# A fused attention and max-out kernel: two PSUM pools to the end, one two-term product instead of three, and new engine shares in the head

## The chip, the cores and the metric

One core of a Trainium2 chip runs the kernel. The metric is the time of one execution on the device, in microseconds (us); the profile's span is some 1.8 us shorter, because it counts from the first to the last instruction. All executions told of here count as fast: none was over 1.5% above the fastest of its kernel. TensorE is called PE, VectorE DVE, ScalarE ACT and GpSimd POOL in the profile's lines.

## The reference

```python
x, state: (8, 8, 512, 64), (8, 8, 32, 64)      # batch, head, sequence, depth
a     = softmax(x @ state^T / 8);   xread = a @ state        # (8, 8, 512, 64)
a2    = softmax(state @ x^T / 8);   sread = a2 @ x           # (8, 8, 32, 64)
X     = concat([xread, sread], sequence), heads side by side # (8 * 544, 512)
out   = maximum(X @ w1, X @ w2) @ w_out                      # w1, w2: (512, 1024), w_out: (1024, 512)
```

The kernel uses two identities. With max(h1, h2) = relu(h1 - h2) + h2, the output is relu(X (W1 - W2)) W_out + X (W2 W_out). And xread = a @ state, so X W = a (state W): for each batch a small matrix SW = state [W1 - W2 | W2 W_out], of 1536 columns in three chunks of 512, replaces the large products. "Layer 1" is aT against the first two chunks with a relu; "layer 2" is aT against the third chunk plus the relu's result against W_out.

## The kernel before

Batch 0 runs while the weights still land. W1 - W2 must be made from fp32 data; where it is not ready, the kernel computes state W1 + (-state) W2 as a product in two terms. Batches 1 to 7 are a steady loop. The parts that matter (cuts marked with #...):

```python
    pools = dict(ps=early.enter_context(tc.tile_pool(name="ps", bufs=4, space=bass.MemoryType.PSUM)),
                 acc=early.enter_context(tc.tile_pool(name="acc", bufs=4, space=bass.MemoryType.PSUM)))
    def one_ring():
        early.close()
        pools["ps"] = pools["acc"] = ctx.enter_context(tc.tile_pool(name="ring", bufs=8, space=bass.MemoryType.PSUM))
#...
    load_states(first)
    load_x(0)
    for ch in range(2):
        load_w(w2f, moe_w2, ch)
        load_wo(2 * ch)
        load_wo(2 * ch + 1)
    load_w(w1f, moe_w1, 0)
    load_w(w1f, moe_w1, 1)
    load_x(1)
    load_states(slice(3, 8))
    load_x(2)
#...
    def sw_mm(b, ch, engs="VA"):
        pg = [bank(), bank()]
        two = b < TWO and ch < 2 and (b, ch) != (1, 0)
        terms = ((sbd, w1b), (sneg, w2b)) if two else ((sbd, wcat),)
#...                                   the head, from W1's second half on
    w_cast(w1b, w1f, 1)
    compact_x(1, 0)
    compact_x(1, 1)
    d_xt(1)
    cast_x(1)
    w_sub(2)
    w_sub(3)
    cast_states("P", rest)
    load_x(3)
    sT = d_states(rest)
    l2_add(0, 0, range(0, 4))
    u_sw(0, 1)
    for c in range(1, NC):
        l2_add(0, c, range(0, 4))
    l1(0, {}, range(4, 8))
    u_sc(1, 0, nc.vector)
    u_sc(1, 1, nc.gpsimd)
    cast_x(2)
    l2_add(0, 0, range(4, 8))
    l2_close(0, 0)
    u_sw(1, 0)
    l2_add(0, 1, range(4, 8))
    l2_close(0, 1)
    u_sw(1, 1)
    u_sr(1)
    compact_x(2, 0)
    compact_x(2, 1)
    l2_add(0, 2, range(4, 8))
    l2_close(0, 2)
    u_at(1, "V")
    l2_add(0, 3, range(4, 8))
    l2_close(0, 3)
    d_xt(2)
    u_sw(1, 2)
    u_srt(1)
    l2_out(0)
    one_ring()
    for b in range(1, B):
        #... steady loop: l1(b), l2(b), and batch b + 1's work between
```

`compact_x` casts x to bf16 on ScalarE, `d_xt` transposes it by DMA, `u_sc` is scores, Exp and normalisation, `u_at` the transpose of the attention weights with its copy out of PSUM (aT), `u_sw(b, ch)` one chunk of SW with its copies (swt), one half on VectorE and one on ScalarE.

The softmax here doesn't subtract the row's maximum and nothing guards it: scores larger than these inputs give would overflow.

## Time and profile before

| | before |
|---|---|
| time, median of the 6 executions beside the changed kernel | 152.12 us (151.97 to 152.38) |
| span of the profiled execution | 150.1 us |
| x of batch 1 landed / its transpose landed | 27.85 / 34.25 us |
| layer 1 of batch 1 starts | 41.94 us |
| a steady batch | 13.97 us (41.94 to 55.91) |

The prediction below shows and reads the main lines. One more, of the view of what each engine waited for, up to 42 us (who, for whom, us in total, times, longest):

```profile
PE ps L311 <- ACT sread_t L68: 0.8, 1, 0.8
```

L311 is layer 1. PE waits there because the two PSUM pools are closed and one pool of eight banks is opened, and the new pool's first bank waits for the old pools' last users.

### The profile page before, as it was taken

Reading aid. Unit: us, or ns where it says so; the run is one execution under the profiler, and the core shown is the slowest. Engines: PE = TensorE matmul, PEld = TensorE weight load, DVE = VectorE, ACT = ScalarE, POOL = GpSimd, SP = SyncE. Lnnn points to the kernel's source line nnn. Section 1 sums busy time; section 2 is a strip of 40 time slices with the busy share of each in tenths; the row PEclk is TensorE's granted clock in tenths of the full one; section 3 lists DMA queues with packets and bytes.
Section 4 is the critical chain, followed back from the end, with each engine's and each line's share of the span. In section 5 each row is a group of like instructions: output and inputs, shape, how many; then the busy total and the mean of one; then the engine's idle time right before and its main releaser. Section 6 shows DMA issues by size and latency. Waiting matters only on the chain.

```text
span 150.1 us, 3012 instructions
## 1 busy us (share of the span) xinstructions
PE 140.0 (93%) x1235; PEld 68.3 (45%) x1255; DVE 82.3 (55%) x151; ACT 75.6 (50%) x126; POOL 43.9 (29%) x44
## 2 busy tenths in 40 slices
PE   6769999999889999999999999999999999999990
PEld 1357643343435445434544444445445434764460
DVE  5378648428968187716854582658067625721120
ACT  3066339927869147727844683478167136521000
POOL 3025119994843520550064017104100500000000
PEclk9977999999999999999999999999999999999999
DMA  4999999989699867974979397851596030502423
GB/s 97 367 392 388 388 384 328 302 157 280 91 273 286 229 127 242 309 148 76 294 265 198 121 292 216 158 226 55 107 109 279 0 74 37 242 0 70 141 105 109
DMA packets 37934, 29.89 MB, mean 199 GB/s; under 512 B 24864, under 2 KB 33312, under 8 KB 37024
## 3 DMA queue, kind: packets, MB, share of 16 engines
q1 hardware_dynamic: 37776, 29.56, 68.9%
q8 instruction: 10, 0.16, 0.4%
q10 hardware_dynamic: 144, 0.13, 0.3%
q14 instruction: 4, 0.03, 0.1%
HBM read 15.20 MB, written 8.91 MB: 161 GB/s over the span
## 4 chain that ended last, share of the span: by engine, by line
PE 70%; DMA 13%; SPq 7%; ACT 3%; DVE 2%; issue 1%
PE acc L326 31%; PE ps L311 16%; DMA xf<-in_x_dram 10%; PE acc L322 8%; SPq L102 4%; SPq L105 3%; PE ps L283 3%; DMA xt<-xc 3%; PE ps L370 2%; PE acc L380 2%; PE ps L221 2%; PE ps L244 1%; PE acc L360 1%; ACT xc L68 1%; PE acc L378 1%
## 5 line engine op out<-in xcount | busy, mean ns | idle before, releaser
L326 PE MATMUL acc<-wo,r 128*128 128x512 bf16 x238 | 57.8, 379 | 0.6 <-issue 0.2
L326 PEld LDWEIGHTS <-r 128*128 128x128 bf16 x248 | 23.9, 98 | 28.8 <-issue 0.6
L301 DVE TENSOR_SCALAR r<-ps 128x512 bf16<-128x512 f32 x32 | 22.1, 692 | 16.3 <-PE ps L311 16.1
L311 PE MATMUL ps<-aT,swt 128*128 128x512 bf16 x127 | 29.0, 379 | 1.0 <-ACT sread_t L68 0.8
L231 POOL TENSOR_TENSOR a<-e,er 128x512 bf16<-128x512 bf16 x13 | 13.4, 1048 | 54.2 <-ACT e L224 27.1
L70 DVE COPY ob<-acc 128x512 f32<-128x512 f32 (+1 forms) x17 | 11.1, 653 | 30.2 <-PE acc L326 29.8
L68 ACT COPY ob<-acc 128x512 f32<-128x512 f32 (+1 forms) x16 | 9.1, 572 | 28.6 <-PE acc L326 18.9
L299 ACT ACTIVATE r<-ps 128x512 bf16<-128x512 f32 x32 | 19.2, 601 | 8.3 <-PE ps L311 7.7
L68 ACT CAST swt<-ps 128x512 bf16<-128x512 f32 x24 | 12.9, 593 | 12.3 <-PE ps L283 12.2
L311 PEld LDWEIGHTS <-swt 128*128 128x128 bf16 x128 | 12.1, 98 | 15.3 <-DVE swt L70 1.3
L322 PE MATMUL acc<-swt,aT 128*128 128x512 bf16 x56 | 16.7, 380 | 0.8 <-issue 0.8
L72 POOL CAST xp<-xf 128x2048 bf16<-128x2048 f32 (+1 forms) x8 | 14.1, 1768 | 10.2 <-DMA xf<-in_x_dram 10.2
L70 DVE CAST swt<-ps 128x512 bf16<-128x512 f32 x24 | 15.3, 681 | 1.8 <-PE ps L283 1.7
L68 ACT CAST xc<-xf 128x1024 bf16<-128x1024 f32 x14 | 13.9, 1051 | 0.1
L228 DVE TENSOR_REDUCE es<-e 128x16 f32<-128x512 bf16 x16 | 10.6, 662 | 1.8 <-ACT e L224 1.8
L389 POOL TENSOR_TENSOR wcat<-w1f,w2f 128x1024 bf16<-128x1024 f32 x4 | 9.8, 2473 | 3.0 <-DMA w1f<-in_moe_w_dram 3.0
L224 ACT ACTIVATE e<-ps 128x512 bf16<-128x512 f32 x16 | 8.8, 595 | 1.3 <-PE ps L221 0.6
L322 PEld LDWEIGHTS <-aT 128*128 128x128 bf16 x62 | 4.7, 98 | 6.0 <-issue 2.6
L136 PE MATMUL ps<-warm 128*128 128x512 bf16 x14 | 6.0, 568 | 1.5 <-POOL warm L122 1.3
L415 PE MATMUL acc<-wo,w2t 128*128 128x512 bf16 x31 | 7.2, 379 | 0.1
L283 PE MATMUL ps<-wcat,sbd 64*32 64x512 bf16 x168 | 6.7, 380 | 0.1
L221 PEld LDWEIGHTS <-xt 128*128 128x128 bf16 x128 | 5.0, 101 | 2.9 <-DMA xt<-xc 0.6
(68 smaller groups left out, 104.5 us busy)
## 6 DMA issues: line engine op xcount, KB each, us to landing
xf<-in_x_dram SPq DMA_DIRECT2D x8, 1024.0 KB, 7.6
out_dram<-ob SPq DMA_DIRECT2D x7, 1024.0 KB, 5.0
w2f<-in_moe_w_dram SPq DMA_DIRECT2D x2, 1024.0 KB, 10.0
wof<-in_moe_w_out_dram SPq DMA_DIRECT2D x4, 512.0 KB, 11.3
w1f<-in_moe_w_dram SPq DMA_DIRECT2D x2, 1024.0 KB, 15.3
out_dram<-ob SPq DMA_DIRECT2D x3, 256.0 KB, 2.2
out_dram<-obs SPq DMA_DIRECT2D x8, 64.0 KB, 1.7
s_f<-in_state_dram SPq DMA_DIRECT2D x1, 320.0 KB, 13.8
```

The costliest lines, as they stand in the source:

```text
L68: nc.scalar.copy(o, i)
L70: nc.vector.tensor_copy(o, i)
L72: nc.gpsimd.tensor_copy(o, i)
L228: nc.vector.tensor_reduce(d["es"][:, g], d["e"][:, g].rearrange("p i c n -> p (i c) n"), axis=mybir.AxisListType.X, op=ALU.add)
L231: mul.tensor_mul(d["a"][:, g].rearrange("p c i n -> p i c n"), d["e"][:, g], d["er"][:, g].rearrange("p (i c) -> p i c", i=4).unsqueeze(3) ...
L283: nc.tensor.matmul(pg[g][32 * i:32 * i + 32, :], sneg[gs, b, i, :] if k else sbd[gs, b, 2 * i + g, g, :], w[gs, i, ch * 512:(ch + 1) * 512 ...
L299: nc.scalar.activation(out=o, in_=p, func=ACTF.Relu)
L301: nc.vector.tensor_scalar(o, p, scalar1=0.0, scalar2=None, op0=ALU.max)
L311: nc.tensor.matmul(p, SW[b][:, g, f * 128:(f + 1) * 128], AT[b][:, g, :], start=(g == 0), stop=(g == 1))
L322: nc.tensor.matmul(OB[b][1 + c], AT[b][:, g, c * 128:(c + 1) * 128], SW[b][:, g, FF:WC], start=(g == 0), stop=False)
L326: nc.tensor.matmul(OB[b][1 + c], R[b][:, f, c * 128:(c + 1) * 128], wo[:, f, :], start=False, stop=(f == NF - 1))
L389: nc.gpsimd.tensor_sub(wcat[:, :, cs], w1f[:, :, cs], w2f[:, :, cs])
```

## The change

Its intent is to take work off the head: fewer two-term products on PE, a shorter way from W1's landing to the first SW chunk, VectorE instead of the busy GpSimd for W1b's subtraction, no closing of the pools, more warm-up matmuls so that the clock stays up, and x of batch 0 in two pieces so that casts start earlier. Its core:

```diff
-    pools = dict(ps=early..., acc=early...)         # and one_ring(), all of it
+    pools = {k: ctx.enter_context(tc.tile_pool(name=k, bufs=4, space=bass.MemoryType.PSUM)) for k in ("ps", "acc")}
-    load_x(0)
+    load_x(0, 2)
-        pg = [bank(), bank()]
-        two = b < TWO and ch < 2 and (b, ch) != (1, 0)
+        pg = [bank(kind="acc" if ch == 2 and b > 1 else "ps") for g in range(2)]
+        two = (b, ch) == (0, 0)
#... the head: casts dealt anew, warm_up 6+9+2+2+3+1+2 matmuls instead of 6+5+1+3
-    w_cast(w1b, w1f, 0)
+    for e, i in (("V", slice(0, 2)), ("A", slice(2, 3)), ("P", slice(3, 4))):
+        copy(e, w1b[:, i, 0:512], w1f[:, i, 0:512])
#...
-    w_cast(w1b, w1f, 1)
+    w_sub(2, nc.vector)
+    w_sub(3, nc.vector)
#...
     l2_add(0, 2, range(4, 8))
     l2_close(0, 2)
+    u_sw(1, 2)
     u_at(1, "V")
-    l2_add(0, 3, range(4, 8))
-    l2_close(0, 3)
-    d_xt(2)                     # now right after compact_x(2, 1)
-    u_sw(1, 2)
-    u_srt(1)
+    l2_add(0, 3, range(4, 6))
+    u_srt(1)
+    l2_add(0, 3, range(6, 8))
+    l2_close(0, 3)
     l2_out(0)
-    one_ring()
```

More of the change, by code (lines that the diff above doesn't have):

```diff
@@ L40 @@
     assert D == 64 and Ns == 32 and S == 512 and H == 8 and DM == 512 and B % 4 == 0
-    TWO = 2
     WC = FF + DM
@@ L49 @@
     big = ctx.enter_context(tc.tile_pool(name="big", bufs=2))
-    early = ctx.enter_context(ExitStack())
-    pools = dict(ps=early.enter_context(tc.tile_pool(name="ps", bufs=4, space=bass.MemoryType.PSUM)),
-                 acc=early.enter_context(tc.tile_pool(name="acc", bufs=4, space=bass.MemoryType.PSUM)))
+    pools = {k: ctx.enter_context(tc.tile_pool(name=k, bufs=4, space=bass.MemoryType.PSUM)) for k in ("ps", "acc")}
     ctx.enter_context(tc.manual_schedule())
@@ L60, in acc @@
         return bank(kind="acc")
-    def one_ring():
-        early.close()
-        pools["ps"] = pools["acc"] = ctx.enter_context(tc.tile_pool(name="ring", bufs=8, space=bass.MemoryType.PSUM))
     def copy(eng, o, i):
@@ L125 @@
     nc.vector.memset(sbd, 0.0)
-    sneg = consts.tile([128, TWO, 4, Ns], BF16)
+    sneg = consts.tile([128, 4, Ns], BF16)
     wo = consts.tile([128, NF, DM], BF16)
     wcat = consts.tile([128, 4, WC], BF16)
-    w1b = stage.tile([128, 4, FF], BF16)
+    w1b = stage.tile([128, 4, 512], BF16)
     w2b = stage.tile([128, 4, FF], BF16)
@@ L167, in negate_states @@
             gs = slice(64 * g, 64 * g + 64)
-            negate("V", sneg[gs], sbd[gs, 0:TWO, g::2, g, :])
+            negate("V", sneg[gs], sbd[gs, 0, g::2, g, :])
     sread_t = consts.tile([128, 4, B * Ns], BF16)
@@ L283, in sw_mm @@
                     nc.tensor.matmul(pg[g][32 * i:32 * i + 32, :],
-                                     sneg[gs, b, i, :] if k else sbd[gs, b, 2 * i + g, g, :],
+                                     sneg[gs, i, :] if k else sbd[gs, b, 2 * i + g, g, :],
                                      w[gs, i, ch * 512:(ch + 1) * 512],
@@ L384, in moe_sread, with w_sub @@
                 nc.sync.dma_start(out=out[b * L + S:(b + 1) * L], in_=ob[32 * q:32 * q + 32, t, :])
-    def w_sub(q):
+    def w_sub(q, eng=nc.gpsimd):
         cs = slice(q * 256, (q + 1) * 256)
-        nc.gpsimd.tensor_sub(wcat[:, :, cs], w1f[:, :, cs], w2f[:, :, cs])
+        eng.tensor_sub(wcat[:, :, cs], w1f[:, :, cs], w2f[:, :, cs])
     def w_cast(o, w, ch, engs="VA"):
@@ L415, in w_wo, with w_wo_out @@
             nc.tensor.matmul(WO[i], w2t[:, i, f, :], wo[:, f, :], start=(f == 0), stop=(f == NF - 1))
-        if q == 3:
-            copy("V" if i % 2 else "A", wcat[:, i, FF:WC], WO[i])
+    def w_wo_out(i):
+        copy("V" if i % 2 else "A", wcat[:, i, FF:WC], WO[i])
     def fillers(b):
@@ L445 @@
     states(first)
-    warm_up(5)
-    cast_x(0, (("V", slice(0, 4, 2)), ("A", slice(4, 8, 2)), ("V", slice(1, 4, 2)), ("P", slice(5, 8, 2))))
+    warm_up(9)
+    cast_x(0, (("A", slice(0, 4, 2)), ("V", slice(4, 8, 2)), ("P", slice(1, 4, 2)), ("V", slice(5, 8, 2))))
     u_xt(0, 0, "V")
+    warm_up(2)
     u_xt(0, 1, "A")
     u_exp(0, 0)
+    warm_up(2)
     u_exp(0, 1)
-    w_cast(w2b, w2f, 0, "VV")
+    warm_up(3)
+    w_cast(w2b, w2f, 0, "PA")
+    u_norm(0, 0, nc.vector)
+    u_norm(0, 1, nc.vector)
+    w_t(0, 0, "A")
+    w_t(0, 1, "A")
+    u_sr(0)
     wo_cast(0, "P")
@@ L455 @@
     warm_up(1)
-    w_t(0, 0, "A")
-    w_t(0, 1, "A")
-    u_norm(0, 0, nc.vector)
-    u_sr(0)
-    u_norm(0, 1, nc.vector)
-    negate_states()
-    warm_up(3)
-    for q in range(2):
-        for i in range(4):
-            w_wo(q, i)
+    for i in range(4):
+        w_wo(0, i)
+    u_at(0, "V")
     w_cast(w2b, w2f, 1)
-    wo_cast(2, "P")
+    for i in range(4):
+        w_wo(1, i)
     w_t(1, 0, "V")
     w_t(1, 1, "A")
-    u_at(0, "V")
+    negate_states()
+    wo_cast(2, "P")
+    wo_cast(3, "P")
     u_srt(0)
-    wo_cast(3, "V")
+    warm_up(2)
     for i in range(4):
         w_wo(2, i)
-    w_cast(w1b, w1f, 0)
+    for e, i in (("V", slice(0, 2)), ("A", slice(2, 3)), ("P", slice(3, 4))):
+        copy(e, w1b[:, i, 0:512], w1f[:, i, 0:512])
+    for i in range(4):
+        w_wo(3, i)
+    for i in range(4):
+        w_wo_out(i)
+    u_sw(0, 0)
+    u_sw(0, 2)
     w_sub(0)
     w_sub(1)
-    for i in range(4):
-        w_wo(3, i)
-    u_sw(0, 0)
-    u_sw(0, 2)
     l1(0, {}, range(0, 4))
-    for c in range(NC):
-        l2_open(0, c)
-    w_cast(w1b, w1f, 1)
+    w_sub(2, nc.vector)
+    w_sub(3, nc.vector)
     compact_x(1, 0)
@@ L488 @@
     d_xt(1)
+    cast_states("P", rest)
     cast_x(1)
-    w_sub(2)
-    w_sub(3)
-    cast_states("P", rest)
     load_x(3)
     sT = d_states(rest)
-    l2_add(0, 0, range(0, 4))
+    for c in range(NC):
+        l2_open(0, c)
+    for c in range(NC - 1):
+        l2_add(0, c, range(0, 4))
     u_sw(0, 1)
-    for c in range(1, NC):
-        l2_add(0, c, range(0, 4))
+    l2_add(0, 3, range(0, 4))
     l1(0, {}, range(4, 8))
-    u_sc(1, 0, nc.vector)
-    u_sc(1, 1, nc.gpsimd)
+    u_exp(1, 0)
+    u_exp(1, 1)
+    u_norm(1, 0, nc.vector)
+    u_norm(1, 1, nc.gpsimd)
     cast_x(2)
@@ L505 @@
     u_sw(1, 0)
+    u_sr(1)
     l2_add(0, 1, range(4, 8))
@@ L508 @@
     u_sw(1, 1)
-    u_sr(1)
     compact_x(2, 0)
     compact_x(2, 1)
+    d_xt(2)
     l2_add(0, 2, range(4, 8))
     l2_close(0, 2)
+    u_sw(1, 2)
     u_at(1, "V")
-    l2_add(0, 3, range(4, 8))
+    l2_add(0, 3, range(4, 6))
+    u_srt(1)
+    l2_add(0, 3, range(6, 8))
     l2_close(0, 3)
-    d_xt(2)
-    u_sw(1, 2)
-    u_srt(1)
     l2_out(0)
-    one_ring()
     for b in range(1, B):
```

## The prediction

> **What bounds the kernel now.** I first read the page's share of busy time and its forty slices. TensorE (PE) is busy 140.0 of 150.1 us, with its thin slices at the start and two of 8 tenths further on (the 11th and 12th, 37.5 to 45 us); the share alone says nothing of which part can shrink. So I asked for the busy time of each engine by stretches, cut at the places where the order of work changes.
>
> ```profile
> PE 140.0 (93%) x1235; PEld 68.3 (45%) x1255; DVE 82.3 (55%) x151; ACT 75.6 (50%) x126; POOL 43.9 (29%) x44
> PE   6769999999889999999999999999999999999990
> ...
> 9.00:11.30 2.30, 1.75 (x31) 1.20 (x26) 1.49 (x3) 1.69 (x3) 0.00 (x0) 0.62 1.05 388
> ...
> 24.70:34.25 9.55, 9.40 (x55) 3.88 (x56) 4.26 (x7) 6.34 (x9) 9.20 (x6) 1.00 0.94 233
> 34.25:41.94 7.69, 6.46 (x103) 3.01 (x106) 7.02 (x14) 6.09 (x11) 5.25 (x7) 1.00 0.83 189
> 41.94:56.00 14.06, 13.95 (x128) 6.51 (x131) 8.49 (x17) 7.50 (x12) 5.11 (x5) 1.00 0.93 237
> ```
>
> The columns after the stretch and its length are PE, weight load, VectorE (DVE), ScalarE (ACT), GpSimd (POOL), granted clock, DMA share, GB/s. From 41.94 us, where layer 1 of batch 1 starts, PE is full: a batch takes 14.0 us. I check that by count: 16 matmuls of 512 columns in layer 1, 40 in layer 2, at 0.216 us from start to start (16 took 3.45 us in the chain), are 12.1; scores 0.47, read of the state 0.37 and 0.16, SW 0.77, one transpose 0.06: 13.9 of 14.0. So the last 108.2 us can hardly shrink, and the change leaves their matmuls alone. What can be won lies before 41.94.
>
> Next I read the chain that ended last, in order of time (start, length, what), for the stretch before 41.94.
>
> ```profile
> 12.36 15.49 DMA xf<-in_x_dram
> 27.85 0.02 issue
> 27.87 1.99 ACT xc L68 x2
> ...
> 29.89 4.36 DMA xt<-xc
> 34.25 0.05 issue
> 34.29 0.42 PE ps L221 x8
> 34.72 0.02 issue
> 34.74 0.61 ACT e L224
> 35.34 0.02 issue
> 35.37 0.70 DVE es L228
> ...
> 41.94 3.62 PE ps L311 x16
> ```
>
> The head is not bounded by PE. Batch 1's x lands at 27.85, behind all the weights in one stream at some 385 GB/s; ScalarE compacts it in 1.99; the transposing DMA takes 4.36; only at 34.25 can batch 1's scores start. Then VectorE has a queue with no hole. Its timeline:
>
> ```profile
> 35.37 0.69 DVE L228 TENSOR_REDUCE es<-e 128x16 f32<-128x512 bf16 x1 [0.47 <-ACT e L224]
> 36.09 0.25 DVE L230 RECIPROCAL er<-es 128x16 f32<-128x16 f32 x1
> 36.38 0.69 DVE L231 TENSOR_TENSOR a<-e,er 128x512 bf16<-128x512 bf16 x1
> ...
> 40.60 0.68 DVE L70 COPY aT<-ps 128x1024 bf16<-128x1024 bf16 x1
> 41.20 0.68 DVE L70 CAST swt<-ps 128x512 bf16<-128x512 f32 x1
> ```
>
> It ends at 41.88, and the view of the waits of L311 gives PE idle 0.8 us for a ScalarE copy that ends at 41.90, and the weight load of the same line 1.0 us for VectorE's swt. So 41.94 is x's landing, plus 6.4 us of compaction and transpose, plus 1.1 of scores and Exp, plus 6.5 of VectorE.
>
> **What the Trainium skill says.** "VectorE: DVE Perf Modes", the perf-mode tier table, has tensor_tensor on fp32 in SBUF in 1x mode only, and its errata section gives (N+151)/0.96 ns for it: an estimate of 1.22 us for one W1 subtraction of 1024 elements per partition. The kernel before has no such instruction on VectorE. "GPSIMD Engine Reference", 3.1, finds GpSimd about twice as slow; the trace agrees with 2.35 us for a quiet subtraction there. "SBUF — State Buffer", who interferes with whom: a VectorE instruction in a 2-port mode, or with two SBUF inputs against a GpSimd read, shuts GpSimd out for the whole instruction, or is shut out by it. The trace fits: the GpSimd subtraction that began beside a VectorE cast of 0.69 us took 2.85. "TensorE: Matmul & The Clock Gate", part 1: an idle PE falls to half clock; the clock column shows 0.62 at 9.0 to 11.3.
>
> **The change, part by part.**
> 1. Early order and warm-up. x of batch 0 comes as two DMAs, the casts are dealt out again, and 25 warm-up matmuls take the place of 15. This keeps the clock up near 9 to 13 us. But W1's first half lands at 22.15 before and after: the bytes are the same and in the same order. PE then has only W_out work between, and in the timeline before it ends at 22.8, just after that landing. Worth to the end: 0.
> 2. W1a cast by three engines. Before: two casts, 0.69 on VectorE and 1.04 on ScalarE. After: VectorE 0.69, ScalarE about 0.6 (half as much, from 618 ns for the 512-element cast), GpSimd about 0.55 (half of 1.04). GpSimd and VectorE both want the shared port, so one follows the other: cast ready near 23.4, not 22.85. Behind it, VectorE still has two wcat casts (1.28) and the first swt cast, so layer 1 starts at about 24.7 as now if VectorE gets the port first, 25.2 if not. Worth: 0 to -0.5 here.
> 3. One two-term pass instead of three. Each extra term is 16 half-height matmuls' second half: 24 of them take 0.77, so 8 take 0.26. SW(0,1) and SW(1,1) lose one each: 0.5 us of PE. The w1b casts of the second half (0.85 VectorE, 1.04 ScalarE) go.
> 4. Subtraction of W1b on VectorE, 2 x 1.22 = 2.4, from 27.2, when layer 1's second VectorE relu is done. GpSimd is in its own subtractions until about 28 and then has casts, so by the exclusive port I allow 29.7 to 31.7 for the end. PE reaches SW(0,1) at 24.7 + 8 x 0.216 (layer 1) + 8 (open) and 12 (add) of the same = 30.75. So waits of 0 to 1 us. GpSimd loses 4.66 us of subtraction, none of it on the chain.
> 5. PE at layer 1's second half: 30.75 + 0.26 + 0.86 = 31.9, plus 1.73 = 33.6, before 34.2. That 0.6 is won and lost at once: the scores need xt, which lands at 34.25, and nothing in the change moves x(1)'s landing, its compaction or its transpose.
> 6. From 34.25. PE has 0.47 scores, 16 adds (3.46), 24 SW matmuls (0.77), 0.53 state read, 0.44 transposes, 0.06: 5.7 us, free by 40.0. But VectorE's list is the same thirteen: two reduces, two reciprocals, one multiply, two ob copies, three swt casts, two for sr, aT. Only the order differs; aT is last now. 35.37 + 6.52 = 41.89, and layer 1 needs aT. PE fills what it won with waiting.
> 7. Two PSUM pools to the end. With four banks in each, a bank comes back after four uses: four layer-1 groups take 1.73 us, and the relu takes 0.6 to 0.7; SW's third chunk sits in acc, where a group is 2.16 us. I find no place where a bank would be late in a steady batch. The closing of the two pools before batch 1, where PE now waits for the sread_t copy, goes away, but VectorE holds the same place to 0.05 us. In the stretch before it, four banks and VectorE's late swt copies could hold SW(1,1) and with it VectorE's own next input: 0 to 0.3 us lost.
>
> Sum: 0 from parts 1, 3 and 5 (hidden), 0 to +0.4 from parts 2, 4 and 7 where the 0.6 of slack doesn't take it. I choose +0.05: 152.4 us.
>
> **Rivals.** (a) PE is the bound in the head, and its saved time comes through: 0.5 for two terms, 0.8 for the wait at 41.94, 1.0 more of holes between 34.25 and 41.94. For it: PE is 98% busy from 24.7 to 34.25. Against it: the xt wait at 34.25 and VectorE's full queue. It would give 150.3 to 151. (b) The shared port makes the new VectorE subtractions slow, up to 2.4 each behind GpSimd. Then SW(0,1) waits until 32 or 33, layer 1's second half ends at 35 to 36, and everything follows: 153 to 154. For it: GpSimd is busy 9.20 of the 9.55 us there. Against it: it loses 4.66 us of them, and waits for states to land at about 29. (c) Four banks are too few in the steady batches, 0.1 to 0.2 in each of seven: 153 to 153.7. For it: the author of before joined the pools on purpose. Against it: the count above.
>
> **Range and chances.** Centre 152.4. Half of (a) gives the lower end, 151.2; (b) or (c) in part the upper, 153.2. To be faster by over 2% takes 3.0 us, more than all the holes of the head before 41.94 that could be closed with x landing when it does (3.3 less what VectorE holds): 0.03. Slower by 3 us needs (b) and (c) together: 0.02. Within 2%: 0.95.
>
> **What would show it.** Right: xf of batch 1 still lands near 27.9 and xt near 34.3; a PE wait for xt of about 0.6 in place of the 0.1 now; VectorE without a hole from the first reduce to aT, and layer 1 of batch 1 at 41.8 to 42.4, with aT as its releaser; batches of 14.0. The new subtractions 1.2 us each when undisturbed; over 2 means the port. Wrong: xt landing a microsecond earlier or later, layer 1 of batch 1 before 41.5, or a batch that isn't 14.0.

## The result, and the profile after

The changed kernel takes 151.71 us (median of 6, 151.25 to 151.82) against 152.12: a ratio of 0.9965, 95% interval 0.9947 to 0.9982. A ratio is the mean time of one kernel's fast runs over that of the other's of the same rounds, so not quite the ratio of the medians quoted. Run again on another occasion, it took 151.67 against 152.29, ratio 0.9962 (0.9940 to 0.9985). So it is some 0.35% faster: 0.5 us, inside the range of 151.2 to 153.2, and "the same" at the 2% mark.

The page after, its first line of busy times and PE's forty slices; then the busy times by stretches, cut again at layer 1 of batch 0, at the scores of batch 1, and at layers 1 of batches 1 and 2 (columns as in the prediction):

```profile
PE 139.9 (94%) x1229; PEld 67.7 (45%) x1249; DVE 82.3 (55%) x149; ACT 75.0 (50%) x126; POOL 42.8 (29%) x45
...
PE   6988999999799999999999999999999999999990
```

```profile
24.14:33.71 9.57, 9.22 (x47) 3.78 (x48) 6.36 (x8) 5.35 (x8) 7.02 (x5) 1.00 0.98 241
33.71:41.39 7.68, 6.26 (x97) 3.08 (x99) 6.80 (x14) 5.85 (x10) 3.83 (x5) 1.00 0.71 187
41.39:55.34 13.95, 13.69 (x126) 6.38 (x129) 8.40 (x16) 7.50 (x12) 5.12 (x5) 1.00 0.97 242
```

PE's sum is the same to 0.1 us. The stretches are what to compare: 9.57 against 9.55 before, 7.68 against 7.69, a batch 13.95 against 13.97. Every part of the way from batch 1's scores on has kept its length; the changed kernel is only shifted to the left, by 0.54 us at the scores (34.25 to 33.71) and 0.55 at layer 1 (41.94 to 41.39). So whatever was won was won before 33.71. Layer 1 of batch 0 is shifted as much already (24.71 to 24.14), and so is the landing of W1's first half (22.13 to 21.53): the whole stream of loads came earlier in this run. The chain that ended last shows the stretch between (start, length, what):

```profile
29.36 4.35 DMA xt<-xc
33.71 0.05 issue
33.75 0.42 PE ps L214 x8
...
34.83 0.70 DVE es L221
...
40.74 0.61 DVE aT L63
41.34 0.04 issue
```

Line by line this is the chain of before: transpose (4.35, before 4.36), scores, Exp, VectorE's queue from 34.83. Only its end is another: the queue now ends with aT (40.74 to 41.34), where before an swt copy came last. Two lines of PE's timeline show its waits, in brackets with the releaser:

```profile
33.75 0.64 PE L214 MATMUL ps<-sbd,xt 128*128 128x64 bf16 x16 [0.34 <-DMA xt<-xc]
...
41.39 3.61 PE L306 MATMUL ps<-aT,swt 128*128 128x512 bf16 x15 [0.86 <-DVE aT L63]
```

The 0.8 us that PE spent before for the pools' closing is there again, 0.86, for aT. And the landing of batch 1's x, where the chain starts, is 27.32 in this run, against 27.85: that 0.53 is nearly the whole shift. One profiled run of each can't settle it, because landings differ from run to run, so it needs kernels.

### The profile page after: what moved, and what is told of

The parts are those of the page before. It is cut to its first block, busy times and chain, and to the rows that moved or that the text cites. A ratio compares the mean times of both kernels' runs of the same rounds, so it can differ in the third digit from the quotient of the medians.

```text
span 149.5 us, 2991 instructions
## 1 busy us (share of the span) xinstructions
PE 139.9 (94%) x1229; PEld 67.7 (45%) x1249; DVE 82.3 (55%) x149; ACT 75.0 (50%) x126; POOL 42.8 (29%) x45
## 4 chain that ended last, share of the span: by engine, by line
PE 73%; DMA 13%; DVE 6%; SPq 4%; issue 2%; ACT 1%
PE acc L321 32%; PE ps L306 18%; DMA w1f<-in_moe_w_dram 10%; PE acc L317 9%; DMA xt<-xc 3%; PE ps L365 2%; PE acc L375 2%; PE ps L278 2%; PE ps L214 2%; SPq L98 2%; DVE swt L63 2%; PE acc L355 1%; PE ps L237 1%; PE acc L373 1%; DVE es L221 1%
## 5 line engine op out<-in xcount | busy, mean ns | idle before, releaser
L61 ACT CAST swt<-ps 128x512 bf16<-128x512 f32 x18 | 9.9, 588 | 14.0 <-PE ps L278 14.0
L63 DVE CAST swt<-ps 128x512 bf16<-128x512 f32 x18 | 11.7, 680 | 1.2 <-PE ps L278 1.2
L129 PE MATMUL ps<-warm 128*128 128x512 bf16 x24 | 8.2, 470 | 1.3 <-POOL warm L115 1.3
L214 PE MATMUL ps<-sbd,xt 128*128 128x64 bf16 x128 | 5.2, 193 | 0.9 <-ACT xt L61 0.6
```

The costliest lines, as they stand in the source:

```text
L61: nc.scalar.copy(o, i)
L63: nc.vector.tensor_copy(o, i)
L214: nc.tensor.matmul(p[:, k * 64:k * 64 + 64], d["xt"][:, 4 * i + 2 * g + cp, :], sbd[:, b, 2 * i + g].rearrange("p u n -> p (u n)"), start= ...
```

## The experiments

They ran in four calls, each beside the kernel before on that call's chip (b_pools_split, a_at_first, a_twoterm and a_x_early share their runs of the kernel before with b_split, a_whole, a_mulpool and b_pools). Each had five rounds, 6 runs of the kernel and 11 or 12 of the kernel before. Apart from the first, each was to tell where the 0.35% comes from and where the rest of the work that was taken away went. Of the profiled run, the table gives when batch 1's x landed (x1), its transpose (xt1), and when layer 1 of batches 1 and 2 started.

| kernel | us, median (lowest to highest) | ratio to before (95% interval) | x1 | xt1 | layer 1, batch 1 | batch 2 |
|---|---|---|---|---|---|---|
| before | 152.07 to 152.34, by call | 1 | 27.85 | 34.25 | 41.94 | 55.91 |
| changed | 151.71 (151.25–151.82) | 0.9965 (0.9947–0.9982) | 27.32 | 33.71 | 41.39 | 55.34 |
| a_again | 151.67 (151.50–151.89) | 0.9962 (0.9940–0.9985) | 27.46 | 34.21 | 41.89 | 55.85 |
| b_split | 151.80 (151.58–151.93) | 0.9965 (0.9941–0.9989) | 27.48 | 34.02 | 41.71 | 55.68 |
| a_whole | 152.09 (151.71–152.58) | 0.9983 (0.9957–1.0008) | 27.90 | 34.29 | 41.98 | 55.93 |
| b_pools | 151.37 (151.23–152.22) | 0.9946 (0.9918–0.9973) | 27.77 | 34.20 | 41.29 | 55.25 |
| b_pools_split | 151.27 (150.93–151.62) | 0.9924 (0.9897–0.9952) | 27.45 | 34.47 | 41.55 | 55.59 |
| a_twoterm | 151.62 (151.41–152.21) | 0.9954 (0.9926–0.9982) | 27.77 | 34.13 | 41.82 | 55.77 |
| a_at_first | 151.39 (151.03–151.50) | 0.9932 (0.9908–0.9955) | 27.71 | 34.16 | 41.25 | 55.59 |
| a_mulpool | 151.30 (151.18–151.54) | 0.9933 (0.9910–0.9956) | 27.41 | 34.06 | 40.97 | 55.31 |
| a_x_early | 151.62 (151.19–151.84) | 0.9951 (0.9927–0.9975) | 24.57 | 31.12 | 40.83 | 55.67 |
| a_simple | 151.55 (151.16–151.70) | 0.9948 (0.9924–0.9971) | 27.64 | 34.37 | 40.75 | 55.71 |
| a_best | 151.28 (150.86–151.73) | 0.9932 (0.9905–0.9959) | 24.68 | 31.17 | 41.86 | 55.84 |
| a_fetch | 151.37 (150.83–152.30) | 0.9951 (0.9915–0.9986) | 27.64 | 34.33 | 41.16 | 56.41 |

The last four columns are one run each; the profiled run of a_fetch was its slowest, and that of the kernel before was on the fast side of its runs (span 150.1 us; the 11 of a call have medians of 150.3 to 150.6). So small differences in these columns are read only where several kernels agree.

### a_again: the changed kernel itself once more

> The changed kernel once more, unchanged, on the same chip and beside the same runs of the kernel before as the two others of this call. Expected by all theories: 0.3 to 0.7 us under the kernel before.

Measured: 0.9962, as the first time. The gain is real and small. In this profiled run x1 landed at 27.46 but its transpose only at 34.21, and layer 1 started at 41.89.

### b_split and a_whole: x of batch 0 in two DMAs, alone and taken out

```diff
# b_split: the kernel before with
-    load_x(0)
+    load_x(0, 2)
# a_whole: the changed kernel with
-    load_x(0, 2)
+    load_x(0)
```

> The kernel before with one edit: batch 0's x comes as two DMAs of 512 KB. Theory 1 (the gain is the earlier landing of batch 1's x, and the split of batch 0's x brings it, because the slowest of the 16 DMA engines then lags by 0.75 us and not by 1.3 when that x has landed, and every later landing carries the lag on): x of batch 1 lands 0.4 to 0.6 us earlier than in the kernel before, layer 1 of batch 1 starts at 41.3 to 41.6, time 0.3 to 0.5 us under the kernel before. Theory 2 (the gain is PE work saved by the dropped second terms and the missing wait at the pool's closing): no difference, within 0.1 us. Theory 3 (landings differ from execution to execution, the split has nothing to do with it): no difference on the mean, within 0.15 us.

> The changed kernel with one edit taken back: batch 0's x as one DMA of 1 MB. Theory 1: x of batch 1 lands near 27.8, layer 1 of batch 1 starts at 41.8 to 42.1, the time is that of the kernel before within 0.15 us. Theory 2: it stays 0.4 to 0.5 us faster than the kernel before. Theory 3: it stays as fast as the changed kernel on the mean.

Measured: this one argument gives the kernel before 0.9965, as much as the whole change; without it the changed kernel is at 0.9983, and its interval holds 1. All else in the change together is then worth at most some tenths of a per cent, and perhaps nothing; but that interval holds 0.9965 too, so "most of the gain" is the likeliest reading and not a proof. The landings agree: in the nine profiled runs with x of batch 0 in two pieces and the loads behind it in the old order, x1 landed at 27.54 on average (27.32 to 27.77), in the three with it whole at 27.84 (27.77 to 27.90). In b_split itself x1 came 0.37 us sooner, for 0.4 to 0.6 expected, and layer 1 started at 41.71, not within the 41.3 to 41.6 expected.

The next step of that path is not shown, though. The transpose of batch 1's x landed at 34.16 on average in the nine runs and at 34.25 in the three: of the 0.30 us at x1, only 0.08 is left. The three runs with x whole were the fastest or second fastest of their kernel in the call, so these few profiles can't settle it. That the split makes the kernel faster rests on the times; how its gain reaches the end stays open.

In b_split layer 1's wait is still that of before, in PE's timeline:

```profile
41.71 3.62 PE L311 MATMUL ps<-aT,swt 128*128 128x512 bf16 x16 [0.83 <-ACT sread_t L68]
```

Why two pieces of the same bytes let the stream end 0.3 us sooner stays open. The idea I had, that the slowest DMA engine falls less far behind the first within x of batch 0, fits two runs (1.32 us behind in before, 0.75 in the changed kernel) and is contradicted by others: in a_mulpool it was 1.51 behind and x1 still landed at 27.41, and in b_pools, with x whole, only 0.96.

### b_pools and b_pools_split: the PSUM pools alone, and with the split

```diff
# b_pools: the kernel before with
-    early = ctx.enter_context(ExitStack())
-    pools = dict(ps=early..., acc=early...)     # and one_ring() and its call
+    pools = {k: ctx.enter_context(tc.tile_pool(name=k, bufs=4, space=bass.MemoryType.PSUM)) for k in ("ps", "acc")}
-        pg = [bank(), bank()]
+        pg = [bank(kind="acc" if ch == 2 and b > 1 else "ps") for g in range(2)]
# b_pools_split: b_pools with load_x(0, 2)
```

> The kernel before with the two PSUM pools of four banks kept to the end (and the third SW chunk of batches 2 on in the accumulators' pool), nothing else. Prediction on record: the wait for the sread_t copy at batch 1's layer 1 goes, VectorE holds the same place to 0.05 us, and no bank is late in a steady batch: time within 0.15 us of the kernel before, batches of 14.0. If four banks are too few: batches of 14.1 or more, 0.7 us or more slower in all. If the closing of the pools cost its 0.8 us of idle PE: 0.4 to 0.8 faster.

> The kernel before with two parts of the change alone: the two pools to the end, and batch 0's x in two DMAs. If the two gains are independent (pools 0.65 us between aT and layer 1 of batch 1, split 0.2 to 0.5 us at x's landing): 0.9 to 1.3 us under the kernel before, and so faster than the whole changed kernel by some 0.5 us. If they overlap: no better than the pools alone (some 1.0 under).

Measured: 0.9946 and 0.9924. The pools alone are worth 0.5%, at least as much as the whole change (the intervals overlap), though the prediction gave them nothing. That the split adds to them isn't shown: these two intervals overlap as well. VectorE's timeline of b_pools, and PE's layer 1 beside it:

```profile
40.56 0.68 DVE L64 COPY aT<-ps 128x1024 bf16<-128x1024 bf16 x1
41.15 0.68 DVE L64 CAST swt<-ps 128x512 bf16<-128x512 f32 x1
```

```profile
41.29 3.62 PE L305 MATMUL ps<-aT,swt 128*128 128x512 bf16 x16 [0.22 <-DVE aT L64]
```

Layer 1 starts at 41.29, 0.05 us after aT is done, while VectorE still copies the third chunk of SW until 41.83. Layer 1 doesn't read that chunk, layer 2 does. Before, the closing of the pools made layer 1 wait for those copies too; with it gone, the path is shorter by one copy, 0.6 us. The changed kernel also drops the closing, but it moves the third chunk ahead of aT and so puts the copy back on the path. No bank is late in the batch that follows: with four banks in each pool it takes 13.96 us, from 41.29 to 55.25, where the kernel before takes 13.97.

### a_at_first: aT ahead of the third chunk, in the changed kernel

```diff
     l2_close(0, 2)
-    u_sw(1, 2)
     u_at(1, "V")
+    u_sw(1, 2)
```

> The changed kernel with batch 1's aT made before its third SW chunk, as the kernel before had it. Theory 1 (the change gave the pools' gain back by putting aT last in VectorE's hole-free queue): layer 1 of batch 1 starts right after aT, 0.6 us earlier after xt's landing (7.1 us and not 7.7), the time 0.4 to 0.6 us under the changed kernel, 0.9 to 1.1 under the kernel before. Rival (the third chunk's cast or another engine holds the same place): no difference, within 0.1 us.

Measured: 151.39, ratio 0.9932, against 0.9965 and 0.9962 of the changed kernel: 0.3 us less, for 0.4 to 0.6 expected. Layer 1 starts 7.09 us after xt1 (34.16 to 41.25), not 7.68. But the win isn't carried on whole. The next lines of PE's timeline:

```profile
41.25 3.61 PE L306 MATMUL ps<-aT,swt 128*128 128x512 bf16 x15 [0.23 <-DVE aT L63]
...
45.07 0.64 PE L214 MATMUL ps<-sbd,xt 128*128 128x64 bf16 x16 [0.21 <-ACT r L294]
```

Batch 1 takes 14.34 us here (41.25 to 55.59) and not 13.95. The second line, batch 2's scores, starts 3.82 us after layer 1, where it is 3.45 in the changed kernel (41.39 to 44.84): 0.37 of the 0.39 is lost right there. The bracket names a relu on ScalarE, but PE's weight load of the same line waited 0.7 us for the DMA that transposes batch 2's x, up to 45.07. That transpose lands between 44.2 and 45.9 in all kernels and becomes the next thing that is late.

### a_mulpool: one multiply taken from VectorE's queue

```diff
-    u_norm(1, 0, nc.vector)
+    u_norm(1, 0, nc.gpsimd)
```

> The changed kernel with one multiply of batch 1's softmax (0.69 us) moved from VectorE to GpSimd, which is idle then. If VectorE's hole-free queue from the first reduce to aT sets the start of batch 1's layer 1: that queue ends 0.6 us earlier, layer 1 of batch 1 starts near 40.8 and not 41.4, and the time falls 0.5 to 0.6 us below the changed kernel (some 0.9 to 1.1 below the kernel before). If PE's own work set it: no difference, within 0.1 us.

Measured: 151.30, ratio 0.9933; layer 1 at 40.97, 6.91 us after xt1. So VectorE's queue did set layer 1: taking 0.69 us off it moved layer 1 by 0.77 against xt1. Of this, 0.39 is lost again at once: batch 1 takes 14.34 us, and the view of waits has 0.7 us of PE's weight load for batch 2's xt.

### a_twoterm: the dropped products put back

```diff
-        two = (b, ch) == (0, 0)
+        two = b < 2 and ch < 2 and (b, ch) != (1, 0)
-    w_sub(2, nc.vector)
-    w_sub(3, nc.vector)
+    w_cast(w1b, w1f, 1)
     compact_x(1, 0)
     #...
-    cast_states("P", rest)
     cast_x(1)
+    w_sub(2)                    # on GpSimd, as before
+    w_sub(3)
+    cast_states("P", rest)
```

> The changed kernel with three passes in two terms, W1b's casts and its subtraction on GpSimd, as the kernel before had them. Prediction on record: the 0.5 us of PE work and the 4.66 us of GpSimd are off the path, hidden behind xt's landing and VectorE's queue: time of the changed kernel within 0.15 us. If PE bounds the head: 0.4 to 0.6 us slower.

Measured: 151.62, ratio 0.9954, the changed kernel's within the noise. The three two-term passes and the subtraction on GpSimd cost nothing at the end: layer 1 of batch 1 is 7.69 us after xt1 (34.13 to 41.82), as in the changed kernel (7.68). In PE's timeline the scores of batch 1 start with no wait worth printing, where the changed kernel waited 0.34:

```profile
34.18 0.64 PE L214 MATMUL ps<-sbd,xt 128*128 128x64 bf16 x16
```

So PE's saved half microsecond had been spent waiting for xt.

### a_x_early and a_best: batch 1's x ahead of W1's second half

```diff
# a_x_early: a_at_first with
     load_w(w1f, moe_w1, 0)
-    load_w(w1f, moe_w1, 1)
     load_x(1)
-    load_states(slice(3, 8))
-    load_x(2)
+    load_w(w1f, moe_w1, 1)
#... compact_x(1), d_xt(1), then these two loads, ahead of w_sub(0); cast_x(1) ahead of cast_states;
#... Exp of batch 1 ahead of layer 1's second half, one multiply on GpSimd; compact_x(2), d_xt(2) earlier
# a_best: a_x_early with cast_x(1) on ScalarE alone, and compact_x(2), d_xt(2) right after batch 1's normalisation
```

> The changed kernel rearranged after the theory that batch 1's x, its transpose and VectorE's queue set the start of batch 1's layer 1: x of batch 1 loaded before W1's second half, its compaction and transpose before the last loads, its scores before layer 1's second half of batch 0, aT before the third SW chunk, one multiply on GpSimd, batch 2's compaction earlier. Theory 1: x of batch 1 lands near 24.4, xt near 31, layer 1 of batch 1 starts at 38.8 to 39.6 (it starts at 41.4 in the changed kernel), time 1.8 to 2.5 us under the changed kernel. If PE in truth bounds the head: less than 0.5 us gained. If the second half of W1 (3 us later) or the last loads become the bound: layer 1 of batch 0's second half waits, 0 to 1 us gained.

> The rearranged kernel a_x_early with two mends of what its trace showed: ScalarE makes batch 1's xp, so that GpSimd reads nothing from SBUF while VectorE subtracts W1b; batch 2's compaction and transpose come before batch 1's SW chunks. If the shared port made the two subtractions 2.07 us each there (GpSimd's cast beside them 2.84 and not 1.9): they take 1.2 to 1.3 us each, the SW chunk that waits for them starts near 30.3 and not 31.4, layer 1 of batch 1 at 38.9 to 39.6, no wait for batch 2's xt, time 1.6 to 2.3 us under the changed kernel. If the port had nothing to do with it: subtractions stay at 2 us, and the time is within 0.5 us of the changed kernel.

Measured: 0.9951 and 0.9932, 0.1 and 0.4 us under the changed kernel where some 2 were expected. xt1 came 3 us sooner in both, at 31.1 and 31.2, and the end hardly moved. In a_x_early VectorE's two subtractions of W1 ran beside a GpSimd cast:

```profile
27.18 4.13 DVE L382 TENSOR_TENSOR wcat<-w1f,w2f 128x1024 bf16<-128x1024 f32 x2 [0.37 <-DMA w1f<-in_moe_w_dram]
```

```profile
27.39 2.84 POOL L65 CAST xp<-xf 128x2048 bf16<-128x2048 f32 x1
```

The two took 4.13 us, and PE waited 0.97 for them before SW(0,1). In a_best GpSimd is quiet there and the same two take 2.49. But now ScalarE has nothing to compact, because batch 2's x, whose load was issued only at 29.90, landed only at 36.98. ScalarE's timeline and PE's:

```profile
37.09 1.99 ACT L61 CAST xc<-xf 128x1024 bf16<-128x1024 f32 x2 [2.87 <-DMA xf<-in_x_dram]
```

```profile
39.62 0.61 PE L253 MATMUL ps<-ident,a 128*128 128x128 bf16 x8 [1.34 <-ACT swt L61]
```

ScalarE's copy of swt stands behind that compaction, and PE waits 1.34 us for it. But 3 us could not be won here at all. From layer 1 of batch 0 to that of batch 1 PE is busy for 15.48 of 17.25 us in the changed kernel (view of the stretch 24.14 to 41.39), so it has only 1.8 us of idle time to give. In a_x_early it is 15.41 of 16.66, and batch 1's scores start at 32.57, with no wait, 1.45 us after xt1: there PE is what is late. So of the 1.8 us, 1.0 is lost to the slow subtractions in a_x_early and 1.3 to the late load in a_best, and in a_x_early batch 1 then takes 14.84 us: layer 1 of batch 2 starts at 55.67 and 55.84, as in the other kernels.

### a_simple and a_fetch: batch 2's transpose earlier, and a fetch moved

```diff
# a_simple: a_at_first with the multiply on GpSimd, as in a_mulpool, and
     u_sw(1, 0)
+    compact_x(2, 0)
+    compact_x(2, 1)
+    d_xt(2)
     u_sr(1)
#... and not after u_sw(1, 1)
# a_fetch: a_simple with warm_up(9) -> warm_up(5) and three warm_up(2) removed
```

> The changed kernel with three moves in its queues: batch 1's aT before its third SW chunk, one multiply from VectorE to GpSimd, batch 2's compaction on ScalarE right after the first SW chunk, so that batch 2's transposing DMA starts 1.6 us earlier. Theory (VectorE's queue of batch 1, then batch 2's xt, are the bounds one after the other): layer 1 of batch 1 starts at 40.1 to 40.5, PE does not wait for xt of batch 2, batch 1 takes 13.95 us, time 0.9 to 1.2 us under the changed kernel. If batch 2's xt was not what took back the gain of the earlier runs: 0.3 to 0.5 as there.

> The kernel a_simple with 10 of its 25 warm-up matmuls left out, 20 instructions of PE. Theory: in a_simple the DMA engines fetched PE's next 16 KB of instructions at 41.38 us, in the middle of batch 2's transposing DMA, which then stood still for a microsecond (DMA share 0.07 from 42 to 43 us) and landed 6.3 us after its issue and not 4.4; with 20 instructions fewer in front the same fetch comes some 2 us later, at 43.0 to 43.8, behind the transpose. Then xt of batch 2 lands 4.2 to 4.9 us after its issue, PE waits for it 0 to 0.2 us and not 0.82, and the time is 0.5 to 0.9 us under a_simple, 150.6 to 151.0. If the fetch has nothing to do with it: the transpose takes 6 us again and the time is that of a_simple within 0.2 us. If the warm-up matters to the end: slower than a_simple.

Measured: 0.9948 and 0.9951, no better than a_mulpool; a_simple's 0.9 to 1.2 us under the changed kernel became 0.2. In a_simple layer 1 of batch 1 starts at 40.75, the earliest of all, and batch 1 then takes 14.96 us, because the transpose of batch 2, issued at 38.9 and not at 40.0, took 6.3 us. The view of that tile in a_simple, and then in the changed kernel, ends with:

```profile
DMA to landing us min/median/max: 6.3/6.3/6.3
```

```profile
DMA to landing us min/median/max: 4.2/4.2/4.2
```

A fetch of PE's instructions (a queue of its own in the trace, ten fetches, one for each 256 of PE's instructions) started at 41.38, within it, and the window from 42 to 43 us has a DMA share of 0.07, with 7 GB/s: that transpose, which still had 2 us to go, nearly stood still. A fetch also started between the issue and the landing of batch 2's transpose in a_x_early, at 40.02, and in a_best, at 43.03; these transposes took 6.0 and 6.2 us. In the ten kernels of the table other than these three and a_fetch, the transpose took 4.2 to 4.6. A fetch came there too, but before the transpose's issue or at most 0.5 us after it (39.92 for an issue at 39.96 in the changed kernel, 40.51 for 40.47 in a_again), when little or none of its data has moved: a_again has a DMA share of 0.00 from 41.0 to 41.5.

a_fetch has 20 fewer of PE's instructions ahead, to move the fetch behind the transpose; it came at 42.65, sooner than I had worked out, still within, and the transpose took 6.6. So the experiment missed its aim. All four transposes with a fetch that started 0.9 us or more after their issue are slow, and the ten others are not; that the fetch is the cause is not shown. A rival fits as well, and no run separates the two: the four slow ones were issued, at 38.86 to 39.27, while the transposing DMA of the states (sT) was still under way, to 40.19 at the least; the ten others were issued after it had landed. PE's wait in a_fetch:

```profile
45.90 0.64 PE L214 MATMUL ps<-sbd,xt 128*128 128x64 bf16 x16 [1.12 <-DMA xt<-xc]
```

With these warm-ups gone, PE's clock in a_fetch's profiled run fell to 6 and 5 tenths in the third and fourth slices of the page (mean clock 0.977), and batch 1's scores started at 34.84, 0.5 us after their x. This was its slowest run, 152.30; the other five, at 0.999 or more, average 151.31. So a clock as low as that may cost something, on the evidence of one run. Less of it shows no such cost: of the kernel before's 34 different runs that are recorded with a clock, the 15 at 0.995 or more average 152.33 us, the 19 at 0.99 or less 152.13.

## Why the prediction was right, and where it was wrong

It said 152.4 with a range of 151.2 to 153.2 and 0.95 for "within 2%"; measured are 151.71 and 0.35% less than before. It named a gain of nothing (0.05 us slower) and got 0.5 us, which its range allowed for but its steps did not. By its own signs it was off as well: layer 1 of batch 1 at 41.39 in the profiled run is before the 41.5 that it called wrong, though in a_again it is 41.89, as said. Step by step:

- **Part 1** was wrong in one piece. The warm-ups show no gain, as said (the kernel before is no faster in its runs at a full clock), though no run takes the added ones alone away from the changed kernel. But "the bytes are the same and in the same order" is no reason for the same landing: x of batch 0 in two DMAs brings x1 0.30 us forward on average, and b_split shows the end moving by 0.35%. By a_whole this is most or all of what the change gained; how it gets from x1 to the end isn't shown.
- **Part 2** held. W1's first half landed at 21.53, layer 1 of batch 0 started at 24.14, 2.61 us later; before, 2.58 (22.13 to 24.71). VectorE's cast went first and took 0.69; GpSimd's, beside it, took 1.14 where I had put 0.55: that size was off, with no effect.
- **Part 3** held: a_twoterm puts the half microsecond of PE back and the time stays.
- **Part 4** held: the two subtractions took 2.88 us and were done at 29.57, just under my 29.7 to 31.7; PE went through at 30.29 without a wait.
- **Part 5** held in kind. PE's wait for xt is there, 0.34 in the one profiled run and 0.70 in the other, for 0.6 predicted. "Nothing in the change moves x(1)'s landing" fell with part 1.
- **Part 6** held to the hundredth: VectorE's queue took 34.83 to 41.34, 6.51 us for 6.52, with aT last and layer 1 released by it. a_mulpool shows that this queue is the bound: shorten it and layer 1 moves.
- **Part 7** was half wrong. Batches take 13.95, so four and four banks are enough, as said. But "VectorE holds the same place to 0.05 us" took the end of VectorE's queue for the end of what layer 1 needs. With the closing of the pools gone, layer 1 needs aT only, not the third chunk's copy behind it: 0.6 us, which b_pools shows. The change itself gave it away by its new order, and a_at_first takes it back. So the prediction for this change came out right in part by luck: the pools' gain that it overlooked and the cost of the new order, which it did not count either ("only the order differs"), cancel. For the pools alone, its gain of nothing would have been wrong by 0.5%.

Of the rivals, (a), PE as the bound, is refuted by a_twoterm for this change, though a_x_early shows that it is near: with x out of the way, PE is the late one. (c) is refuted by the batches of 13.95. (b), slow subtractions beside GpSimd, was slight in the changed kernel (2.88 us for the two, against 2.49 in a_best) and made PE wait for nothing; a_x_early shows that it can, with 4.13 and 0.97 of waiting.

What would have been a larger gain at this place is cut off by the next one: between kernels, layer 1 of batch 1 starts anywhere from 40.75 to 41.98, and that of batch 2 at 55.25 to 56.41, in several of them because batch 2's transpose lands only at 44.2 to 45.9 us. b_pools_split, a_best, a_mulpool and a_at_first are the fastest by their ratios, some 0.7% under the kernel before and 0.3% under the changed one; the differences between them are within their intervals.

## What to carry to other kernels

Count an engine's queue only up to the instruction that the waiting one reads: what stands behind that in the queue costs nothing, and one item moved ahead of it costs its whole length. Work taken off an engine that waits a little later for a load only lengthens that wait, so look for the wait first, and then for the wait that comes after it. The idle time of the busiest engine caps what an earlier load can bring: 1.8 us here, for a load that came 3 us sooner. A DMA's landing in a full stream isn't fixed by bytes and order alone: cut it differently and measure, over several runs.

## What the Trainium skill lacked or had wrong

- "Runtime: NRT & Kernel Launch", "Instruction fetch mechanics", says that instructions come in blocks of 256 by a DMA queue of the sequencer's own and that crossing a block costs "one DMA tail-bump, mostly hidden". The trace agrees with the blocks (ten fetches for PE's some 2500 matmuls and weight loads). It doesn't say what a fetch does to data on the way. The landings fit a fetch that takes a place on one of the 16 DMA engines of the data: the one at 15.55 us in the kernel before took 1.13 us, and from then on the last engine was 1.08 to 1.15 us behind the fifteenth in each of the loads behind it (0.08 in the load before), down to x1. That is one profile read after the fact, and no experiment.
- "DMA: Bandwidth & Descriptors", "Why a DMA increments its semaphore by 16 and not by 1", says that the engines finish independently and only the full count means that all has landed. The trace agrees, and gives the size: x1's first engine was done at 25.50 us in the kernel before, its last at 27.85. The page has nothing on how cutting a load in two changes the landing of those behind it (0.30 us here, unexplained).
- No page says what an instruction fetch does to a transposing DMA in flight: 6.0 to 6.6 us in four runs where one started 0.9 to 3.9 us after the transpose's issue, 4.2 to 4.6 in ten where it came earlier; a coincidence so far, not a shown cause, since another transpose in flight separates the same runs.
- "SBUF — State Buffer", who interferes with whom, is right in kind and gives no size for this pair (VectorE tensor_tensor against a GpSimd cast): a VectorE subtraction of 1024 elements per partition took 2.10 us on average beside a GpSimd cast and 1.28 without, the latter close to the 1.22 estimated from "VectorE: DVE Perf Modes"; the GpSimd cast took 2.84 beside it, and 1.88 elsewhere.
